# Two moves where the first pass over an image meets the second: the first reloads of x go behind the last read of a normalized block, and the recomputed and kept g are given the places ahead of x's

## The chip, the cores and the metric

The kernel runs on one core of a Trainium2 chip. The metric is the device time of one execution in microseconds. An execution has five engines that run side by side: PE (matrix products), ACT (activations), DVE (elementwise work and statistics), POOL (elementwise work, and the issue of some transfers) and SP (the issue of most transfers).

## What is computed

The reference is one ConvNeXt-V2 block on an image of 512 x 512 pixels with 96 channels, in bfloat16:

```python
out = sum over i, j in 0..2 of xp[:, i:i+H, j:j+W, :] * dw[i, j]     # depthwise 3x3, zero padding
h = _layernorm(out, axis=-1)                                         # over the 96 channels
h = gelu(einsum('bhwc,ce->bhwe', h, w1))                             # 96 -> 384, tanh form
gx = sqrt((h * h).sum(axis=(1, 2), keepdims=True) + 1e-6)            # over all pixels
nx = gx / (gx.mean(axis=-1, keepdims=True) + 1e-6)
h = grn_gamma * (h * nx) + grn_beta + h
return x + einsum('bhwe,ec->bhwc', h, w2)                            # 384 -> 96
```

What matters for the shape of the kernel is `gx`: it sums over all 262,144 pixels, so no output can be made before the last pixel has gone through the gelu. The kernel folds the scale `1 + grn_gamma * nx` into `w2` (the tile `W2s`) and the rest into one row (`B2c`).

## The kernel before

**Blocks.** The image is cut into 128 blocks of four rows (`GR = 4`, `NBLK = 128`), 2048 pixels each. There are two passes over the blocks.

**First pass** (the loop over slots, lines 844 to 986). A block goes through stages in successive slots: x is loaded (`load_x`, SP), transposed on DVE into `xT`, convolved on PE, moved to `y_bf` by ACT; its layer norm factor is worked out; POOL multiplies it in (`stage_norm`, line 639, tile `yn`); SP writes the normalized block to memory in four transfers (`stage_write`, line 647) and in the next slot reads it back with the channels on partitions (`stage_read`, line 652) into one of six buffers `ynT0` to `ynT5`. Two slots later comes its MLP: products with `w1` on PE, gelu on ACT into a tile called g, and the sums of g squared, partly by statistics on DVE (`bst`) and partly by Gram products on PE (g times its own transpose, `gram_next`, line 770, whose diagonal is read at the end). The Gram products of a unit are issued some units later, out of the list `grams`.

So a slot that runs the MLP of block m issues on SP the read of block m + 2 and then the writes of block m + 3 (lines 857 to 861); the last read, of block 127, belongs to the slot `last_slot - 2`.

**Where g stays.** 35 blocks write g to memory (`g_dram`). Six blocks, `HELD` (114, 116, 118, 120, 122, 125), keep g in on-chip memory for the second pass: five in the pool `g`, and 125 in the pool `gh`. The other blocks drop g and have it recomputed in the second pass from the normalized block. Four of these, `KEPT` (123, 124, 126, 127), keep their `ynT` buffer, so that they need not be read again. In the first pass the dropped g of late blocks lies in tiles that have become free: that of 123 over `xin`, that of 124 over `xT` (`overs`, line 274, used in `mlp_tail`, line 677), and those of 126 and 127 in the pool `gr`, which serves the second pass too.

**The end of the first pass.** The last 14 blocks (`mlp_tail`) have no convolution beside them. A block is four units; a unit is products into three banks of PSUM and one gelu of 128 x 1536. PE alternates between two sets of three banks, so unit u waits for the gelu of unit u - 2. After the slot of block 124 (`s == last_slot - 3`, line 975) the eight pools of the convolution are closed (`pc.close()`) and the pools of the second pass are opened in their place, from the right end of the memory: `xr` (x again, five buffers of 3,072 bytes per partition), `gr` (three of 12,288), `gh` (one of 12,288), `gld` (g read back, two of 12,288) and `o` (outputs, six of 3,072). Right there SP gets the reloads of x for the first four blocks of the second pass (`load_xr`, lines 982 and 983, `XPRE = 4`). The tiles that had this place, from the right end, are: `xin` (13,824 bytes per partition), `xT` (17,280), `y_bf` (thirteen of 3,072), `ysq`, some small ones, `rbc` and `yn`. An instruction that first writes into a new pool waits for the last users of all old tiles under that pool.

**Between the passes** (lines 989 to 1034): the remaining Gram products, the sums on DVE, a short chain of tiny operations, and `W2s`. PE and ACT meanwhile recompute g for the first blocks (`advance`).

**Second pass** (lines 1044 to 1056), in the order `ORDER`: 123, 124, 126, 114, 127, 1, 0, and so on, recomputed blocks mixed with kept and reread ones. Per block: recomputed g where needed (PE, ACT), eight groups of products with `W2s` on PE, and per group DVE adds `B2c`, per two groups DVE adds x (`xr`). POOL issues the reload of x for the block four places ahead (first of these at n = 0, line 1047) and the reads of g; SP issues the reads of normalized blocks and the outputs.

**Order of the work.** All engines keep the order in which the program calls them (`InOrder`, line 25) up to n = 8 of the second pass. So a transfer on SP that waits holds all those behind it. In the profile most operations of the first pass have one line, 35, that of the recording helper; tiles tell them apart.

Of the kernel before, what the change touches and what calls it, by code (L numbers as in the profile page):

```python
# [56 lines left out]
def kernel(  # L57
# [127 lines left out]
    p2 = ExitStack()  # L185
    SL = PXP + 2
    with ExitStack() as p1:
# [93 lines left out]
        def load_xr(n, pq):  # L281
            q = ORDER[n]
            r0 = q * GR
            xr = late.xr.tile([128, PXP, C], bf16, name="xr")
            pq.dma_start(out=xr[:], in_=x[0, r0:r0 + GR].rearrange("r w c -> (r w) c").rearrange(  # L285
                "(p g) c -> p g c", g=PXP))
            grp.setdefault(q, {})["xr"] = xr
# [523 lines left out]
        for k, (b0, n) in enumerate(BATCHES):  # L811
# [16 lines left out]
            for b in range(b0, b0 + n):  # L828
# [8 lines left out]
                last_slot = m  # L837
# [6 lines left out]
        for s in range(last_slot + 1):  # L844
# [129 lines left out]
                combine(b)  # L974
            if s == last_slot - 3:
                pc.close()
                late.xr = p2.enter_context(tc.tile_pool(name="xr", side="right", bufs=5))
                late.gr = p2.enter_context(tc.tile_pool(name="gr", side="right", bufs=GRB))
                late.gh = p2.enter_context(tc.tile_pool(name="gh", side="right", bufs=1))
                late.gl = p2.enter_context(tc.tile_pool(name="gld", side="right", bufs=2))  # L980
                late.o = p2.enter_context(tc.tile_pool(name="o", side="right", bufs=6))
                for n in range(XPRE):
                    load_xr(n, sp)
            if s == last_slot:
# [102 lines left out]
```

## Time and profile before

| what | value |
| --- | --- |
| median of three runs | 1464.99 us (1461.61, 1464.99, 1469.38) |
| the profiled execution's own time | 1464.07 us |
| its span in the profile | 1462.3 us |
| mean granted clock of PE | 0.992 |
| busy, share of the span: PE | 1390.5 us, 95% |
| ACT | 1399.1 us, 96% |
| DVE | 1317.4 us, 90% |
| POOL | 901.3 us, 62% |
| moved by DMA | 421.26 MB, mean 288 GB/s |
| first output products | 967.3 us from the start |

How to read it. The span is the stretch from the first to the last instruction of the profiled execution; its own time, 1.8 us longer, is the device time of the same execution. Busy time of an engine is the union of its instructions; "granted clock" is the share of full speed that PE was allowed. In a timeline a row is a group of like instructions that follow each other: start, duration of the group, engine, line, operation, tile written <- tiles read, count, and in brackets how long the engine stood idle before it and what ended that. SPq is the queue of transfers that SP issues: its rows show the issue, not the transfer. In the rows of stretches each engine has its busy time and count of instructions, in the order PE, weight loads, DVE, ACT, POOL; then come the granted clock, the share of the DMA engines' time, and GB/s.

### The profile page before, as it was taken

The numbers are of one execution on the slowest core, as the hardware profiler recorded it, in microseconds if no ns is written. First come the engines' busy times: TensorE is split into PE (matmuls) and PEld (weight loads), VectorE is DVE, ScalarE is ACT, GpSimd is POOL, SyncE is SP. The second block draws the span as 40 slices with busy tenths as digits, with TensorE's granted clock in tenths as the row PEclk, the third lists the DMA queues.
The fourth block names the chain that finished last, engine by engine and source line by source line (L and its number), as shares of the span: only waits on it lengthen the run. The fifth ranks groups of instructions, "written<-read, shape, count | busy, mean of one in ns | idle before, by whom it ended". The sixth has DMA issues, their size and how long they took to land.

```text
span 1462.3 us, 54717 instructions
## 1 busy us (share of the span) xinstructions
PE 1390.5 (95%) x23128; PEld 812.5 (56%) x23128; DVE 1317.4 (90%) x2422; ACT 1399.1 (96%) x1591; POOL 901.3 (62%) x796
## 2 busy tenths in 40 slices
PE   8889999999999999999999997699999999999998
PEld 3444444444444444444444444467777777777776
DVE  7749999999999999999999998668888888888888
ACT  6879999999999999999999999889999999999997
POOL 2559999999999999999999998201111111111111
PEclk9999999999999999999999999999999999999999
DMA  6577899898888898889889877539999999999997
GB/s 194 157 212 232 254 264 275 260 265 265 267 245 263 271 273 261 273 263 256 268 252 269 247 244 211 163 132 372 370 334 371 395 406 402 403 411 413 390 416 304
DMA packets 167275, 421.26 MB, mean 288 GB/s; under 512 B 34198, under 2 KB 83798, under 8 KB 162550
## 3 DMA queue, kind: packets, MB, share of 16 engines
q1 hardware_dynamic: 151508, 313.80, 67.3%
q0 software_dynamic: 14960, 103.82, 18.3%
q8 instruction: 181, 2.97, 0.9%
q14 instruction: 64, 0.52, 0.1%
q10 hardware_dynamic: 562, 0.15, 0.1%
HBM read 261.38 MB, written 156.22 MB: 286 GB/s over the span
## 4 chain that ended last, share of the span: by engine, by line
PE 42%; DVE 27%; ACT 15%; DMA 9%; issue 3%; POOL 2%; SPq 1%; ACTq 0%; POOLq 0%; DVEq 0%
PE PS L35 42%; DVE bst L35 19%; ACT g L35 9%; DVE xT L35 5%; ACT y_bf L35 3%; DMA ynT<-yn_dram 3%; DMA yn_dram<-yn 2%; DMA rbc<-r_dram 1%; SPq L35 1%; DMA out_dram<-o_sb 1%; DMA xin<-in_x_dram 1%; ACT xT L35 1%; POOL yn L35 1%; DVE y_bf L35 1%; DVE o_sb L35 1%
## 5 line engine op out<-in xcount | busy, mean ns | idle before, releaser
L35 ACT ACTIVATE g<-PS 128x512 bf16<-128x512 f32 (+2 forms) x1046 | 708.0, 838 | 9.1 <-PE PS L35 5.9
L35 DVE BATCH_NORM_STATS2 bst<-g 128x6 f32<-128x512 bf16 x1086 | 659.0, 673 | 22.5 <-ACT g L35 22.3
L35 ACT ACTIVATE gr<-PS 128x1536 bf16<-128x1536 f32 x356 | 493.1, 1451 | 19.1 <-PE PS L35 14.0
L35 POOL TENSOR_TENSOR yn<-y_bf,rbc 128x1536 bf16<-128x1536 bf16 x126 | 390.8, 3104 | 53.1 <-ACT rbc L35 23.1
L35 PE MATMUL PS<-ynT,w1p 128*128 128x512 bf16 x1170 | 335.6, 382 | 30.4 <-DMA ynT<-yn_dram 6.6
L35 PE MATMUL PS<-xT,Wq 64*32 64x511 bf16 (+1 forms) x9198 | 346.4, 390 | 16.7 <-ACT y_bf L35 5.0
L35 DVE TENSOR_TENSOR o_sb<-PS,B2c 128x384 bf16<-128x384 f32 x512 | 280.9, 557 | 67.6 <-PE PS L35 62.2
L35 POOL TENSOR_TENSOR ysq<-y_bf 128x1536 bf16<-128x1536 bf16 x114 | 312.8, 2744 | 24.1 <-ACT y_bf L35 17.6
L35 PE MATMUL PS<-ynT,w1s 128*128 128x512 bf16 x996 | 269.2, 379 | 3.9 <-DMA ynT<-yn_dram 3.3
L285 POOL DMA_DIRECT2D xr<-in_x_dram x116 | 62.2, 536 | 294.8 <-DVE o_sb L35 294.8
L35 PEld LDWEIGHTS <-gr 128*128 128x128 bf16 x4248 | 209.6, 98 | 56.8 <-issue 1.5
L35 PE MATMUL PS<-W2s,gr 128*128 128x96 bf16 x4176 | 218.9, 206 | 0.5 <-DVE o_sb L35 0.4
L35 PEld LDWEIGHTS <-Wq 64*32 64x32 bf16 x9216 | 113.2, 91 | 180.6 <-issue 136.9
L35 ACT ACTIVATE y_bf<-PS 128x1536 bf16<-128x1536 f32 (+2 forms) x135 | 182.9, 1360 | 19.7 <-PE PS L35 19.6
L35 PEld LDWEIGHTS <-w1p 128*128 128x128 bf16 x1170 | 90.1, 98 | 186.5 <-issue 108.4
L35 DVE STREAM_TRANSPOSE xT<-xin 128x576 f32<-128x576 f32 (+1 forms) x256 | 181.5, 749 | 4.4 <-PE PS L35 4.3
L35 DVE TENSOR_TENSOR o_sb<-o_sb,xr 128x768 bf16<-128x768 bf16 x256 | 142.9, 558 | 8.9
L35 PEld LDWEIGHTS <-g 128*128 128x128 bf16 (+1 forms) x1611 | 98.0, 98 | 84.0 <-issue 53.4
L35 PE MATMUL PS<-w1p,ynT 128*128 128x256 bf16 (+2 forms) x828 | 126.8, 274 | 9.3 <-ACT g L35 2.7
L35 PE MATMUL PS<-g 128*128 128x128 bf16 x1368 | 114.6, 220 | 1.3 <-DVE PS L35 1.3
L35 PEld LDWEIGHTS <-w1s 128*128 128x128 bf16 x996 | 79.7, 98 | 43.9 <-issue 3.7
L35 PEld LDWEIGHTS <-gl 128*128 128x128 bf16 x1680 | 82.5, 98 | 23.1 <-issue 0.9
(115 smaller groups left out, 757.5 us busy)
## 6 DMA issues: line engine op xcount, KB each, us to landing
xin<-in_x_dram SPq DMA_DIRECT2D x126, 432.0 KB
g_dram<-g SPq DMA_DIRECT2D x105, 512.0 KB
gl<-g_dram POOLq DMA_DIRECT2D x35, 1536.0 KB, 9.4
yn_dram<-yn SPq DMA_DIRECT2D x512, 96.0 KB
ynT<-yn_dram SPq DMA_DIRECT2D x128, 384.0 KB
out_dram<-o_sb SPq DMA_DIRECT2D x127, 384.0 KB
xr<-in_x_dram POOLq DMA_DIRECT2D x124, 384.0 KB, 7.4
ynT<-yn_dram SPq DMA_DIRECT2D x249, 128.0 KB
```

Source lines behind the costliest of these rows:

```text
L35: r = f(*a, **k)
L285: pq.dma_start(out=xr[:], in_=x[0, r0:r0 + GR].rearrange("r w c -> (r w) c").rearrange("(p g) c -> p g c", g=PXP))
```

## The change

The pools of the second pass are opened in the order `gr`, `gh`, `xr`, `gld`, `o` instead of `xr`, `gr`, `gh`, `gld`, `o`, still after the slot `last_slot - 3`. From the right end, `gr` then covers bytes 0 to 36,864 (before: 15,360 to 52,224), `gh` 36,864 to 49,152 (52,224 to 64,512) and `xr` 49,152 to 64,512 (0 to 15,360); `gld` and `o` keep their places. And the four first reloads of x are issued after the slot `last_slot - 2` instead of `last_slot - 3`, so that on SP the read of block 127 stands ahead of them.

```diff
             if s == last_slot - 3:
                 pc.close()
-                late.xr = p2.enter_context(tc.tile_pool(name="xr", side="right", bufs=5))
                 late.gr = p2.enter_context(tc.tile_pool(name="gr", side="right", bufs=GRB))
                 late.gh = p2.enter_context(tc.tile_pool(name="gh", side="right", bufs=1))
+                late.xr = p2.enter_context(tc.tile_pool(name="xr", side="right", bufs=5))
                 late.gl = p2.enter_context(tc.tile_pool(name="gld", side="right", bufs=2))
                 late.o = p2.enter_context(tc.tile_pool(name="o", side="right", bufs=6))
+            if s == last_slot - 2:
                 for n in range(XPRE):
                     load_xr(n, sp)
```

On SP the order after the writes of block 127 was: four reloads of x, read of block 127, three reads of block 1. It becomes: read of block 127, four reloads, three reads of block 1. The order on the other engines is the same as before.

## Prediction

> **What bounds the kernel now.** I read the page first, then the busy time in short stretches, then the timelines of SP, PE and POOL around the one dip, the waits, and the chain. The page's rows of forty slices (36.6 us each) find the place:
>
> ```profile
> PE   8889999999999999999999997699999999999998
> PEclk9999999999999999999999999999999999999999
> GB/s 194 157 212 232 254 264 275 260 265 265 267 245 263 271 273 261 273 263 256 268 252 269 247 244 211 163 132 372 370 334 371 395 406 402 403 411 413 390 416 304
> ```
>
> After its start PE is nine tenths busy but for the 25th and 26th slices (877 to 950 us), where the first pass over the image ends and the second begins; the DMA engines move least in the 26th and 27th, 163 and 132 GB/s. So no resource is short in the dip; something waits. The timeline of SP in that place (start, duration, operation):
>
> ```profile
> 926.14 0.31 SPq L35 DMA_DIRECT2D ynT<-yn_dram  x1
> 926.50 2.47 SPq L35 DMA_DIRECT2D yn_dram<-yn  x4
> 931.02 0.31 SPq L35 DMA_DIRECT2D ynT<-yn_dram  x1
> 931.38 2.49 SPq L35 DMA_DIRECT2D yn_dram<-yn  x4
> 940.59 1.80 SPq L35 DMA_DIRECT2D xr<-in_x_dram  x4
> 942.55 2.82 SPq L35 DMA_DIRECT2D ynT<-yn_dram  x4
> ```
>
> SP alternates: read a normalized block, write the next one. After the writes of block 127 (931.38) four reloads of x come, and only behind them, at 942.55, the read of block 127. The waits view of SP, from 930 to 945 us, says what held SP from 933.87 (931.38 + 2.49) to 940.59:
>
> ```profile
> SPq L35 <- PE PS L35: 6.7, 1, 6.7
> ```
>
> The last matmuls on PE before 940.59 are the Gram products of block 124 (`xT`, 940.01 + 0.50 = 940.51), whose g lies where the pool `xr` is put. On PE that read is waited for:
>
> ```profile
> 940.71 0.81 PE L35 MATMUL PS<-w1p,ynT 128*128 128x384 bf16 x6 [0.20 <-ACT gh L35]
> 942.10 0.81 PE L35 MATMUL PS<-w1p,ynT 128*128 128x384 bf16 x6 [0.57 <-ACT gr L35]
> 943.44 0.82 PE L35 MATMUL PS<-w1p,ynT 128*128 128x384 bf16 x6 [0.53 <-ACT gr L35]
> 944.09 0.50 PE L35 MATMUL PS<-gr 128*128 128x128 bf16 x6
> 951.21 1.46 PE L35 MATMUL PS<-ynT,w1p 128*128 128x512 bf16 x3 [6.62 <-DMA ynT<-yn_dram]
> ...
> 953.74 1.49 PE L35 MATMUL PS<-w1p,ynT 128*128 128x384 bf16 x6
> ...
> 955.66 1.06 PE L35 MATMUL PS<-w1p,ynT 128*128 128x384 bf16 x6
> ...
> 956.89 0.82 PE L35 MATMUL PS<-w1p,ynT 128*128 128x384 bf16 x6
> ```
>
> The first three rows are the last units of block 126, one each 1.34 to 1.39 us; the last four are block 127's. PE stands 6.62 us, and afterwards the same matmuls take 1.46 instead of 0.81. The stretches of 2 us show why: the granted clock (eleventh figure, behind POOL's) is 0.50 until 956.
>
> ```profile
> 948.00:950.00 2.00, 0.00 (x0) 0.00 (x0) 0.00 (x0) 0.00 (x0) 0.00 (x0) 0.50 0.99 226
> 954.00:956.00 2.00, 2.00 (x14) 1.47 (x13) 1.81 (x4) 0.89 (x2) 0.00 (x0) 0.50 0.03 8
> ```
>
> Nothing else can run in that hole: ACT and DVE are at 0.00 too, and the second pass needs the sum over all blocks. The chain of waits passes through it: SP until 942.39, then 8.62 us for this read, then PE.
>
> **The change part by part.** No instruction of PE, ACT, DVE or POOL is added, removed or reordered; SP has the same transfers, with the read of block 127 ahead of the four reloads.
>
> *The wait that goes.* The new place of `xr` is 49,152 to 64,512 bytes from the right end: inside the old `y_bf` (31,104 to 71,040), whose last reader is POOL's norm of block 127, 921.61 + 3.08 = 924.69. So the reloads no longer wait for block 124's Gram products, and none stands ahead of the read. The read then waits only for its own block's writes. The three reads before it were issued 1.95, 1.75 and 2.05 us after the last of the four writes (for example 931.02 - 928.97); so 933.87 + 1.9 = 935.8, 6.8 us earlier.
>
> *How long the read then takes.* The trace has no such read with only four reloads behind it, so two bounds. High: 8.62 us as now, with four reloads ahead in the queue and POOL's beside it; it lands at 944.4. Low: a yn write in the chain, 3.08 us; 938.9. When is it needed? After block 126's last unit at 943.44, one pitch later, 943.44 + 1.34 = 944.78. Both bounds lie before that, so I take nothing for either end, and PE doesn't stop. It is close at the high end: cover 0.4 us.
>
> [...]
>
> *The sum.* Block 127's four units start at 944.78, 946.12, 947.46 and 948.80 instead of 951.21, 953.74, 955.66 and 956.89. The last is 8.09 us earlier: 6.43 of wait (951.21 - 944.78), and 1.66 of slow clock (5.68 us between first and last start, against 3 x 1.34 = 4.02). Then come 30 Gram products (PE done 1.68 us after that unit, 959.39 - 957.71) and 12 that wait for the last gelu. ACT would end that gelu at 946.08 + 4 x 1.37 = 951.56, against 959.55: 7.99 earlier. The later of the two releases the last 12 products, so **8.0 us** is what arrives at the scale of W2 (now 966.17) and at the first output matmul (967.31).
>
> *What is late next?* DVE's statistics of block 127 run 3.9 us (954.19 to 958.07) from the end of the first gelu; moved to 947.55 they end by 951.5, still before the last Gram products at 952.4. The reloads: first used at 969.96, so 962.0 afterwards; issued at 936.2 to 938.0 and, with the 10.6 us that all took now (940.59 to the read's landing), there by 947. Nothing.
>
> *POOL's reload.* POOL's first reload (941.16) has the same new place and waits only for the last norm: 924.7. Its 0.39 MB then fall among the writes of 126 and reads of 125 and 126. At 245 GB/s (927 to 929 us) that is 1.6 us. Block 125's read (926.14) is used at 934.00 and 126's (931.02) at 939.37: slack 7.9 and 8.3 less the read itself. I take nothing; if the writes of 127 move too, by 1.6, the read lands at 946.0 at the high bound, and 1.2 us of the gain go.
>
> *The moved pools.* `gr` now covers the old `xin`, `xT` and part of `y_bf`, with `gh` in `y_bf`. In both orders block 126's first gelu waits for the same product of block 124 (940.51), and ACT runs without a gap there (934.92 to 946.08). PE's first Gram product of 126 gets one more wait row, for an x load long past; no more than the 0.05 us the chain shows as "issue".
>
> *The second pass* starts from W2 and moves as a whole: its first transfers (SP's output at 973.23, POOL's gl at 974.05) wait for DVE's output. So 1464.07 - 8.0 = **1456.0 us** for this execution (span 1462.3, 1.8 outside it). The median of the three runs, 1464.99, is 0.9 above it, which allows as much here.
>
> **The rivals.**
>
> *The read lands late all the same* (0.17). POOL's early reload pushes the writes, and the reloads share the engines: 1 to 2 us of wait remain, at full clock. Gain 6.0 to 7.0: 1457.6. For it: 0.4 us of cover at the high bound. Against: the engines carry 0 to 31 GB/s from 935 to 939 us.
>
> *The second pass gives it back* (0.13). Its DMA share is 0.97 to 1.02 and, if that sets its pace, an earlier start only finds the queue full earlier:
>
> ```profile
> 1100.00:1200.00 100.00, 100.00 (x1472) 74.52 (x1471) 85.90 (x159) 98.84 (x72) 18.21 (x34) 1.00 1.01 389
> 1300.00:1400.00 100.00, 99.38 (x1465) 74.06 (x1463) 84.72 (x157) 98.12 (x72) 18.22 (x34) 1.00 1.01 405
> ```
>
> PE is 99 to 100% busy at full clock in them, and waits for DMA data only 3.3 us after 985. Half the gain lost: 1460.
>
> *Slower: the place of gr costs ACT* (0.06). Gelus into `xin` and `xT`, where gr moves, have means of 1562 and 1563 ns, those into gr 1451. Were the place the cause, 356 x 111 ns = 39.5 us come on top: 1495.5. The gain is used up from 8.0/356 = 22 ns each. Against: four in a row into xT, gh and gr take 5.69, 5.74 and 5.48 us, pitches of 1.34 to 1.36, so the longer rows overlap; weight loads from all of them take 98 ns.
>
> *The reload isn't moved off the path*: excluded, since the order on SP puts the read ahead.
>
> **How the numbers follow.** Forecast 1456.0 with 0.64; the rivals 0.17, 0.13, 0.06. About 0.5% (7.3 us) is what a measurement of this kernel can tell from no change, and my 8.0 is only just more: the three runs spread by -3.4 and +4.4 about their median. Of the forecast's 0.64 some 0.58 is on the faster side; of the late read 0.04. So faster 0.62, same 0.32, slower 0.06. Range: 1456.0 - 3.4 = 1452.6 down to 1452; up, half the gain lost (1460) and some of the spread: 1461.5.
>
> **What would show it.** Right: SP's read of 127 near 936, ahead of the reloads; PE's wait for `ynT` under 0.5 us; granted clock 1.00 from 944 to 958; W2 scaled near 958; the second pass as long as now (966.17 to the end). Wrong: a wait for `ynT` of 1 us or more, gr gelus over 1.47 us with a longer pitch, or a second pass longer by microseconds.

## The result and the profile after

Nine runs of each: 1454.06 us median (1450.85 to 1458.90) against 1463.46 (1457.93 to 1470.34). The ratio is 0.9935, 95% interval 0.9909 to 0.9961: 9.5 us faster, between 5.7 and 13.3. The forecast was 1456.0 in a range of 1452.0 to 1461.5.

The profiled execution of the changed kernel took 1458.11 us, its span is 1456.3. SP's timeline, from the writes of block 127:

```profile
929.43 2.49 SPq L35 DMA_DIRECT2D yn_dram<-yn  x4
935.63 0.31 SPq L35 DMA_DIRECT2D ynT<-yn_dram  x1
935.98 1.85 SPq L35 DMA_DIRECT2D xr<-in_x_dram  x4
```

The read of block 127 is issued at 935.63, ahead of the reloads; before it was 942.55, behind them. PE, from block 126's last unit to block 127's last:

```profile
943.46 0.82 PE L35 MATMUL PS<-w1p,ynT 128*128 128x384 bf16 x6 [0.52 <-ACT gr L35]
...
944.81 0.81 PE L35 MATMUL PS<-ynT,w1p 128*128 128x512 bf16 x3 [0.20 <-ACT gr L35]
...
946.15 0.81 PE L35 MATMUL PS<-w1p,ynT 128*128 128x384 bf16 x6
...
947.49 0.81 PE L35 MATMUL PS<-w1p,ynT 128*128 128x384 bf16 x6 [0.19 <-ACT gr L35]
...
948.84 0.82 PE L35 MATMUL PS<-w1p,ynT 128*128 128x384 bf16 x6 [0.19 <-ACT gr L35]
```

No wait for `ynT` is left (in brackets stands what ended an idle time), and the four units start at 944.81, 946.15, 947.49, 948.84; the forecast had 944.78, 946.12, 947.46, 948.80. The stretches of 2 us show the clock at 1.00 (before: 0.50), and ACT (the fourth busy time) running through:

```profile
946.00:948.00 2.00, 1.81 (x24) 1.44 (x21) 0.77 (x2) 2.00 (x3) 0.00 (x0) 1.00 0.00 0
```

DVE starts to scale W2 at 957.51 instead of 965.59, 8.08 us earlier. The span is only 6.0 us shorter, because in this pair of executions the second pass, from that point to the end, took 498.8 us against 496.7. So the profiled execution ended 2.1 us above the forecast that was made for it, 1456.0.

### The profile page after: what moved, and what is told of

The parts are those of the page before. It is cut to its first block, busy times and chain, and to the rows that moved or that the text cites. A ratio compares the mean times of both kernels' runs of the same rounds, so it can differ in the third digit from the quotient of the medians.

```text
span 1456.3 us, 54718 instructions
## 1 busy us (share of the span) xinstructions
PE 1388.1 (95%) x23128; PEld 812.0 (56%) x23128; DVE 1317.4 (90%) x2422; ACT 1399.4 (96%) x1591; POOL 901.7 (62%) x796
## 4 chain that ended last, share of the span: by engine, by line
PE 37%; DVE 36%; ACT 10%; DMA 8%; POOL 4%; issue 3%; SPq 1%; ACTq 0%; POOLq 0%; DVEq 0%
PE PS L35 37%; DVE bst L35 26%; DVE xT L35 7%; ACT g L35 5%; DMA ynT<-yn_dram 3%; DMA yn_dram<-yn 2%; DMA out_dram<-o_sb 2%; ACT y_bf L35 2%; POOL yn L35 2%; ACT gr L35 1%; SPq L35 1%; DVE y_bf L35 1%; POOL ysq L35 1%; DVE o_sb L35 1%; ACT xT L35 1%
## 5 line engine op out<-in xcount | busy, mean ns | idle before, releaser
L35 ACT ACTIVATE gr<-PS 128x1536 bf16<-128x1536 f32 x356 | 493.1, 1451 | 13.1 <-PE PS L35 8.0
```

Source lines behind the costliest of these rows:

```text
L35: r = f(*a, **k)
```

## The experiments

The first pass drifts by some microseconds between executions (block 126's last unit starts between 938.89 and 943.46 us in the thirteen profiles), so profiles are compared by stretches: A from the start of block 126's last unit to that of block 127's first unit on PE, B from there to W2, and C from the start of the scaling of W2 to the end of the span. A row of the table names a run; the headings below say what it is.

| profile | A | B | A + B | C |
| --- | --- | --- | --- | --- |
| before | 7.77 | 14.38 | 22.15 | 496.7 |
| e4_before_again | 6.01 | 13.81 | 19.82 | 499.6 |
| e11_probe_before | 8.04 | 13.96 | 22.00 | 497.9 |
| after | 1.35 | 12.70 | 14.05 | 498.8 |
| e8_after_again | 1.34 | 12.71 | 14.05 | 505.6 |
| e5_probe_after | 1.34 | 12.71 | 14.05 | 507.0 |
| e1_order_only | 1.35 | 12.70 | 14.05 | 504.4 |
| e10_probe_order_only | 1.34 | 12.71 | 14.05 | 502.5 |
| e2_places_only | 1.35 | 12.70 | 14.05 | 500.1 |
| e7_places_again | 1.34 | 12.71 | 14.05 | 497.7 |
| e6_probe_places_only | 1.34 | 12.71 | 14.05 | 496.5 |
| e3_warm_hole | 8.37 | 12.37 | 20.74 | 499.0 |
| e9_more_ahead | 2.91 | 13.88 | 16.79 | 500.3 |

**The order alone** (`e1_order_only`: before, with the reloads moved):

```diff
+            if s == last_slot - 2:
                 for n in range(XPRE):
                     load_xr(n, sp)
```

> Old order of the pools (xr at the right end), only the four reloads of x moved behind the last yn read. Theory (the read of block 127 was held by the reloads ahead of it): SP reads block 127 near 935.8 us, the reloads wait until block 124's last Gram product (about 940.5) with nothing behind them that is soon needed; PE waits for ynT under 0.5 us, the last unit of block 127 starts near 948.8, W2 is scaled near 957.5; 8.0 us less than before, as with the whole change (ratio 0.9945). If POOL's early reload (which stays at 941 here) is what stretched the landing of block 127's writes to 3.7 us after the change, the read follows the last write by 1.75 to 2.05 us, near 933.9. Rival (the places of the pools matter): less than half the gain, ratio 0.997 to 1.0.

Ratio 0.9935 (0.9912 to 0.9959), A + B 14.05. The reloads still wait for block 124's Gram products (SP waits 6.8 us for PE), until 936.62 in this execution, but behind the read, and PE's first unit of block 127 waits for ACT only:

```profile
925.11 2.52 SPq L35 DMA_DIRECT2D yn_dram<-yn  x4
929.45 0.31 SPq L35 DMA_DIRECT2D ynT<-yn_dram  x1
936.62 1.80 SPq L35 DMA_DIRECT2D xr<-in_x_dram  x4
...
940.82 0.81 PE L35 MATMUL PS<-ynT,w1p 128*128 128x512 bf16 x3 [0.19 <-ACT gr L35]
```

The order alone brings the whole gain; the places aren't needed for it. The read followed the last write by 1.82 us (929.45 - 927.63).

**The places alone**, twice (`e2_places_only` and `e7_places_again`: the changed kernel without the move):

```diff
-            if s == last_slot - 2:
                 for n in range(XPRE):
                     load_xr(n, sp)
```

> New order of the pools, but the four reloads of x still ahead of the read of block 127 on SP. Theory: the reloads no longer wait for Gram products, so SP issues them right behind block 127's writes (about 932 to 934) and the read at 934 to 936; what is left is the sharing of the DMA engines. With the high bound of the prediction (8.62 us from issue to landing) the read lands at 942.6 to 944.6, PE waits under 0.5 us, and the gain is 7.5 to 8.0 us (ratio 0.9945). Rival (it is the place in the queue that counts): the read is served only after the 1.6 MB of reloads and the wait for ynT is 2 us or more, gain under 6 us, ratio 0.996 to 1.0.

> The run with the places alone once more, beside the changed kernel on the same chip. If half of the gain is really missing: ratio again near 0.997, and 2 to 5 us above the changed kernel; the wait for ynT or the stretch between block 126's last unit and W2 is longer than 14.05 us in this profile. If the first measurement was chance: ratio 0.994 and the stretch is 14.05 us again.

The first time the ratio was 0.997 (0.995 to 0.999), which is what the rival named, but without the rival's wait; the second time it was 0.9933 (0.9911 to 0.9954), on another chip. A + B is 14.05 in all three profiles of kernels with the places alone (the third is `e6_probe_places_only`, below), with no wait for `ynT`. So the missing half of the first measurement was not seen in any profile and did not come back in one repeat. Whether it was chance, the chip, or waits in timed executions that have no profile stays open: in the execution below the read landed only 0.6 us before it was needed.

**The changed kernel again** (`e8_after_again`):

> The changed kernel once more. Theory: ratio 0.9945 within its interval (8.0 us), the stretch from block 126's last unit to W2 14.05 us, no wait for ynT; the read of block 127 follows the last write by 1.75 to 2.05 us if the 3.7 us of the first profile were chance, by 3.5 us or more if POOL's early reload brings them.

Ratio 0.9941 (0.9916 to 0.9965), A + B 14.05, no wait for `ynT`. The read followed the last write by 1.70 us (935.22 - 933.52), so by the expectation the 3.7 us of the first profile were chance.

**When the read lands** (`e5_probe_after` and `e6_probe_places_only`). One tiny copy on POOL, behind its first reload, waits for the read and so shows its landing:

```diff
+            if n == 0:
+                pool.tensor_copy(out=warm[0:1, 0:16], in_=ynts[NBLK - 1][0:1, 0, 0:16])
```

> The changed kernel with one tiny POOL copy of 16 values out of block 127's ynT buffer, so that its start shows when the read has landed (POOL has nothing else to do there). Theory A (the place in the queue counts): the read, ahead of the reloads, lands 3 to 5 us after its issue, some 4 us or more before PE needs it. Theory B (the transfers share the engines): it lands 7 to 8.6 us after its issue, when nearly all 2 MB are through, under 1.5 us before PE needs it.

> New places but reloads ahead of the read (as in the run with the places alone), with the same tiny POOL copy. Theory A: the read lands only behind the reloads, 6 to 8.6 us after its issue, within about 1.5 us of the moment PE needs it, so that executions with a slower transfer wait; that is where half the gain goes. Theory B: it lands as long after its issue as in the changed kernel, within 1 us.

In the changed kernel (SP's read, then POOL's copy and PE's first unit):

```profile
931.59 0.31 SPq L35 DMA_DIRECT2D ynT<-yn_dram  x1
...
935.48 0.19 POOL L35 COPY warm<-ynT 1x16 bf16<-1x16 bf16 x1 [15.86 <-DMA ynT<-yn_dram]
...
940.84 0.81 PE L35 MATMUL PS<-ynT,w1p 128*128 128x512 bf16 x3 [0.19 <-ACT gr L35]
```

With the places alone:

```profile
932.74 2.14 SPq L35 DMA_DIRECT2D ynT<-yn_dram  x4
...
940.38 0.19 POOL L35 COPY warm<-ynT 1x16 bf16<-1x16 bf16 x1 [19.09 <-DMA ynT<-yn_dram]
...
941.01 0.81 PE L35 MATMUL PS<-ynT,w1p 128*128 128x512 bf16 x3 [0.19 <-ACT gr L35]
```

The read takes 3.9 us ahead of the reloads and 7.6 behind them, and is early by 5.4 us and 0.6 us, in one execution of each kernel. The place in the queue counted: with the reloads right behind it, the read didn't wait until they were through. It landed after 3.9 us; in the first profile of the changed kernel the DMA engines had moved 0.86 MB by so long after its issue (220 GB/s from 935.63 to 939.52), and the read with the four reloads is 1.97 MB. How long it takes with nothing behind it no run shows. All these transfers were issued on SP. Even sharing of the engines among them would bring both landings close together, and that is not what 3.9 against 7.6 shows.

**More ahead of the read** (`e9_more_ahead`). The places alone, with one more transfer between the reloads and the read:

```diff
                     load_xr(n, sp)
+                extra = late.gl.tile([128, NQ, NCH, QW], bf16, name="gl")
+                sp.dma_start(out=extra[:].rearrange("p t j w -> p (t j w)"), in_=g_dram[0])
```

> The places alone (reloads ahead of the read), and one more transfer of 1.5 MB (a stored g, read early into a free buffer and not used) between the reloads and the read of block 127. Theory (the place in the queue counts; 0.6 us of cover were left without it): at 370 to 420 GB/s the 1.57 MB take 3.7 to 4.2 us more, so PE waits 3.1 to 3.6 us for ynT, and the stretch from block 126's last unit to W2 grows from 14.05 to about 17.5 us, or up to 2 us more if the clock drops. Rival (the transfers share the engines evenly): the read lands less than 2 us later, a wait under 1.5 us.

SP's timeline, then PE's first unit of block 127:

```profile
927.87 2.79 SPq L35 DMA_DIRECT2D xr<-in_x_dram  x4
930.70 0.48 SPq L35 DMA_DIRECT2D gl<-g_dram  x1
931.49 2.19 SPq L35 DMA_DIRECT2D ynT<-yn_dram  x4
...
942.21 1.46 PE L35 MATMUL PS<-ynT,w1p 128*128 128x512 bf16 x3 [1.76 <-DMA ynT<-yn_dram]
```

The wait is 1.76 us, half of what I expected and more than the rival's. From the first reload's issue to the landing it took 14.34 us (942.21 - 927.87), with the places alone 10.68 (940.38 - 929.70): 3.66 more, close to the 3.7 to 4.2 expected of the transfer and above the rival's bound of 2. But SP was ahead of PE by more in this execution: the reloads were issued 12.8 us before PE needed the block (939.30 + 1.34 - 927.87), there 11.3. So the cover, the time by which the read would have been early, was 0.6 + 1.5 and not 0.6, and 1.57 us of delay were left. The size of the cover changes from one execution to the next.

**PE kept busy in the hole** (`e3_warm_hole`: before, with products of zeros):

```diff
+            if b == NBLK - 1:
+                for _ in range(28):
+                    pe.matmul(PS[:, 6, :], lhsT=zrow[:, :128], rhs=zrow[:], start=True, stop=True)
```

> The kernel before, with 28 products of zeros (about 6 us) on PE in an unused bank of PSUM in front of block 127's first unit, so that PE is busy while it waits; nothing of the computation is left out. Theory (1.66 us of the gain are the slow clock behind the wait): the read lands as before, near 951.2, the granted clock stays 1.00, block 127's units start 1.34 us apart, the last at 955.2 instead of 956.9, W2 is scaled at 964.5 instead of 966.2. Rival (the units behind the wait are slow for another reason): pitches of 2.5, 1.9 and 1.2 us as before.

PE's timeline, the first two units of block 127, and a stretch of 2 us with the granted clock (last but two):

```profile
949.91 0.82 PE L35 MATMUL PS<-ynT,w1p 128*128 128x512 bf16 x3 [1.17 <-DMA ynT<-yn_dram]
...
951.24 0.82 PE L35 MATMUL PS<-w1p,ynT 128*128 128x384 bf16 x6
...
950.00:952.00 2.00, 2.00 (x23) 1.49 (x23) 0.00 (x0) 1.23 (x1) 0.00 (x0) 1.00 0.05 10
```

The units start 1.33, 1.03 and 1.34 us apart instead of 2.53, 1.92 and 1.23; B falls from 14.38 to 12.37, though the wait remains (A is 8.37). So the slow stretch behind the wait was the clock: the first three products of block 127 take 0.82 us at 1.00 here, and 1.46 at 0.50 in the kernel before. The last unit and W2, expected at 955.2 and 964.5, came at 953.61 and 962.28, mostly since block 126's last unit already came 1.90 us earlier in this execution. B is 0.33 below the changed kernel's 12.70: ACT, idle in the hole, started the first gelu 0.86 us after that unit and not 1.2.

**Before, two more profiles** (`e4_before_again` and `e11_probe_before`):

> The kernel before once more, for the spread of its own profile. Theory: W2 is scaled within 0.3 us of 966.2 (the first pass is paced by ACT and by fixed waits), and the second pass, from there to the end, varies by 1 to 3 us from execution to execution, as much as the second pass of the changed kernel was longer (498.2 against 496.1). Rival (the change makes the second pass longer): the second pass of before stays at 496.1 within 0.5 us.

> The kernel before with the tiny POOL copy, a third profile of its hole. Theory: the read is issued behind the reloads after SP's wait for block 124's Gram products and lands 6.9 to 8.6 us later, the copy shows the same moment as PE's first unit of block 127; the stretch from block 126's last unit to W2 is 19.8 to 22.2 us, so that the gain of the change is 5.8 to 8.1 us from execution to execution. Rival: the hole is always the 8.1 us of the first profile, and the 5.8 of the second was chance.

My expectation of W2 at 966.2 fell: it was 958.9 and 962.4, mostly since block 126's last unit came at 939.12 and 940.37 instead of 943.44. The wait for the read was 4.86 and 6.90 us, so the hole costs 5.8 to 8.1 us (A + B less 14.05), not a fixed 8.1. In `e11_probe_before` POOL's copy ran at 948.42 and PE's unit at 948.41, so the copy does show the landing; the read took 8.94 us from its issue, a little more than the 6.9 to 8.6 expected.

**POOL's reload and the writes** (`e10_probe_order_only`):

> Old places, reloads behind the read, with the tiny POOL copy that shows the landing (it stands behind POOL's reload, which waits for block 124's Gram products here, so it can show no landing earlier than that). Theory: the copy runs as soon as POOL's reload is issued, some 4 us ahead of block 127's first unit, since the read has landed by then; and from the first write of block 127 to its read there are 4.3 to 4.6 us, as in the run with the order alone (4.34), where the changed kernel had 6.2 and 5.2, because POOL's reload is not among the writes. Rival for the latter (chance): 5 us or more here too.

The copy ran at 940.73, right behind POOL's reload and without a wait, so the read had landed at least 2.89 us before PE's unit (943.62); 4 us were expected.

From the first write of block 127 to its read there were 5.65 us in this run, though POOL's reload came only at 939.99. The changed kernel has 6.20, 5.20 and 5.79 in its three profiles, and 4.34 came with the order alone (in the second of these, e8, the four writes alone took 3.50 us to issue instead of 2.49). So a gap of this length comes without POOL's early reload too, as the rival has it; that the reload adds nothing isn't shown by so few. What makes the gap longer stays open. It cost nothing here: the cover of 5.4 us was measured with a gap of 5.79.

## Why the prediction was right, step by step

*The wait that goes*: right. It was the order on SP; e1 shows it alone. That the new places would also free the reloads was right too (in e2 they are issued at 932.55, 0.04 us behind the writes), but I had not seen that this alone would do: either part removes the whole wait in every profile of it. Both together give a cover of 5.4 us, where the places alone had 0.6 and the order alone at least 2.9.

*When the read is issued*: 6.8 us earlier was forecast, 6.9 came, by luck. The gap behind the last write was 3.71 us (935.63 - 931.92) and not 1.9, and the writes were issued 1.95 us sooner.

*How long the read takes*: 3.9 us lies between the bounds of 3.08 and 8.62. The high bound was never near here; it is what the read takes behind the reloads (6.9 to 9.3 in the four profiles with the hole, 7.6 with the places alone). With the reloads right behind it, it stayed 4.7 us under that bound.

*The sum*: 8.0 forecast, 8.08 in the first pair. Its two terms, 6.43 of wait and 1.66 of slow clock, came as 6.42 (7.77 - 1.35) and 1.68 (14.38 - 12.70), and e3 took the second away by itself (2.01, since the first gelu starts sooner there). What the sum hides is that it was made against one execution: against e4 the same sum is 5.77, against e11 7.95. So it is in part luck that the forecast of 8.0 lies so near the timed gain. In the four measurements with a ratio near 0.994 the medians lie 8.7 to 9.9 us below before, more than the hole costs in any of three profiles. The first interval, 5.7 to 13.3, takes in both; whether the rest is noise or something that the change does elsewhere isn't shown.

*What is late next*: nothing, as forecast. DVE's statistics of block 127 ended at 951.36, before the last Gram products.

*The moved pools*: gelus into `gr` have a mean of 1451 ns and are busy 493.1 us, as before; the group in the page after:

```profile
L35 ACT ACTIVATE gr<-PS 128x1536 bf16<-128x1536 f32 x356 | 493.1, 1451 | 13.1 <-PE PS L35 8.0
```

The rival that the place costs ACT is gone.

*The second pass gives it back*: the three ratios of the changed kernel and the order alone (0.9935, 0.9941, 0.9935) leave no room for a loss of half. The profiles don't say it as clearly: C is 496.7 to 499.6 in the four with the long wait (e3 among them) and 496.5 to 507.0 in the eight without a wait, 498.3 and 501.6 on average. The largest values go with PE's waits for recomputed blocks' `ynT` there (after 985 us): 8.1 to 11.9 us in all in the three profiles where C is 504.4 or more (e1, e8, e5), 2.9 to 4.8 in the other ten. The smaller differences don't go with them: before and after both have 3.3 us, with C 496.7 and 498.8. The waits views of e8 (C 505.6) and e6 (C 496.5) say, in all, times, longest:

```profile
PE PS L35 <- DMA ynT<-yn_dram: 11.9, 11, 3.1
```

```profile
PE PS L35 <- DMA ynT<-yn_dram: 2.9, 4, 1.6
```

So some of the second pass's waits are ended by transfers, by an amount that changes between executions of one kernel. Whether an earlier start makes it larger stays open: the three large values all lie among the profiles without the long wait, but the timed executions show no such loss. That the second pass moves as a whole, as the prediction had it, held for the medians of the timed executions; from one profile to the next its length changes by up to 10.5 us.

## What to carry to other kernels

Read the queue of the engine that issues transfers as a program: an early prefetch that waits for a buffer holds every transfer behind it, however soon that one is needed, and the engine that starves is another one (in the kernel before SP waited 6.7 us with the reloads, and PE stood for 6.62). Put the transfer that is needed next ahead of the prefetch, or give the prefetch a place that is free. Here the order alone was enough; the free place alone removed the wait in every profile too, but left only 0.6 us to spare where that was measured. The landing time of a transfer (a copy of 16 values on an idle engine shows it: 948.42 in e11, where PE's unit started at 948.41) says how much cover there is. Compare stretches between fixed points of the profile, since whole times vary by more than such a gain: the nine of the kernel before lie 12.4 us apart, and the gain is 9.5.

## What the runs showed of the hardware

The clock dropped after idle times of very different length: 4.5 us after PE's last product in e4, 3.4 in e11, 1.5 in e9 (its last product ended at 940.46, within a wait of 1.76 us) and 1.3 in the kernel before. It came back 3.0 us after PE's restart in e4, 3.3 in e11, 3.2 in e9 and 4.9 in the kernel before. From drop to return it was 0.50 for 3.41 us in e4 (944.73 to 948.14), 3.41 in e9 (941.96 to 945.37), 6.83 in e11 (944.91 to 951.74) and 10.24 in the kernel before (945.90 to 956.14): one, one, two and three times 3.41. These moments are worked out from stretches of 0.5 us, with the clock taken as 1.00 on one side of the change and 0.50 on the other. For the kernel before they are these two (a mean of 0.90 puts the drop 0.40 us behind the start of the stretch):

```profile
945.50:946.00 0.50, 0.00 (x0) 0.00 (x0) 0.50 (x1) 0.50 (x1) 0.00 (x0) 0.90 0.90 344
...
956.00:956.50 0.50, 0.50 (x6) 0.47 (x5) 0.50 (x6) 0.50 (x1) 0.00 (x0) 0.86 0.00 0
```

So in these four traces the time at 0.50 was a whole multiple of 3.41 us, and neither its start nor its end lay at a fixed distance from PE's last product or its restart. In the 3.41 us that ended with the drop PE was busy for 0.00 us in e4, 0.01 in e11, 1.39 in e9 and 1.57 in the kernel before; in e4 the 3.41 us ahead of those had 1.85 and stayed at full clock.

A short wait can thus cost nearly as much again: in e9 1.57 us of delay at block 127's first unit and 1.17 more (13.88 - 12.71) behind it. PE was busy for 41% and 46% of the 3.41 us ahead of the drop in e9 and in the kernel before, and for next to nothing in e4 and e11, so what the drop depends on isn't shown. But a gap well under 3.4 us wasn't safe: in e9 a wait of 1.76 us was enough.
